# A fused attention and two-layer MoE kernel: the soft dispatch of a token tile issued with the routing logits of the next, 12 places for tile outputs, and block exchanges through DRAM done in place

## The chip, the cores and the metric

The kernel runs on one core of one Trainium2 chip. The metric is the device time of one launch in microseconds; the median of 3 runs before the change is 968.15 us.

## The reference

Three stages in float32. Block-causal attention runs over 8 batches, 8 heads, 576 positions and a head width of 64 (blocks of 64). A dense layer pair follows on 4608 tokens, with ELU between, and then a soft mixture of experts with 32 slots:

```python
attn = softmax(where(mask, scale * q @ k.T, -1e9)); x = concat_heads(attn @ v)
h = x @ w_in
x = where(h > 0, h, exp(min(h, 0)) - 1) @ w_out
logits = x @ phi
d = softmax(logits, axis=tokens);  slot_input = d.T @ x
slot_out[e] = relu(slot_input[e] @ w1[e]) @ w2[e]
out = softmax(logits, axis=slots) @ slot_out
```

## The kernel before, in words

The work is 32 **pairs** (two heads of one batch, numbered `n`) and 36 **tiles** of 128 tokens (numbered `i`); four pairs feed four and a half tiles. Nothing is a loop over all of it at run time: each step is recorded with `add` (engine or engines, a guessed duration, what it reads and writes, a key), and `Plan.order` (L126) replays the records once at build time as a list scheduler over guessed durations. It takes ready steps by the smallest key and so fixes the order of instructions on every engine. On the chip the order is static: an instruction that is not ready holds up all that stands behind it on its engine. The calls at the end (L1140 on) give keys: a tile every `T` = 22, pairs from a `base` that `EARLY` moves ahead.

TensorE (PE) works in four arrangements of its array, which the plan calls modes: F (128x128; the main matmuls, transposes, small sums), R (64 rows; attention scores), C (64 columns; attention times V) and D (32 columns; routing logits and dispatch).

**A tile.** `tile_split` halves the activations into high and low parts. `tile_range` (L787, four times with `r` = 0 to 3) does 12 matmuls of 512 columns (L795 to L797), exponent on ACT (L800), two DVE steps (L802, L805), and writes ELU outputs into one of 8 places of 512 columns, `gslot`. The output weights are folded into the routing matrix and the slot inputs (`g @ w_out` is applied after dispatch), so only `g` and its transpose are needed. For tiles below 30 DVE transposes blocks of 32x32 into `TT` (L813). `tile_turn` (L823) then exchanges the blocks: per half a tile one DMA writes `TT` to DRAM and four bring it back, each for 32 partitions, into another buffer `GT`. `tile_routing` (L832) reads `GT`: 16 matmuls in mode D into bank POST. `tile_dispatch` (L847) makes the softmax parts out of them on DVE, ACT and PE (L855 to L886) and at the end issues the dispatch, 4 matmuls in mode D into the same bank (L893), added to `ACC` by DVE (L897).

**A pair.** Pairs from 8 on transpose the attention weights in two ways (`pair_swap`, L668). DVE transposes 256 columns of each of six units (L678) into `TU`; one DMA to DRAM and four back exchange the blocks into `PX`. The other blocks, 13 of 128x128, are transposed by PE (L359) in four groups, into PSUM banks PTB and GTB in turn, and copied out by ACT or DVE (L335, L337). `swapped_values` (L723) multiplies by V in mode C (L734), 16 matmuls over 1600 columns, counted for both heads side by side.

The tail (from L931) loads the expert weights in pieces of 1 MB into slots that attention, tiles and first-layer weights give back.

Of the kernel before, what the change touches and what calls it, by code (L numbers as in the profile page):

```python
# [28 lines left out]
TLAG, LATE, NTP = 2.5, 30, 8  # L29
EARLY = 8.0  # L30
# [208 lines left out]
def attention_moe_kernel(ctx: ExitStack, tc, q, k, v, w_in, w_out, phi, w1, w2, consts, out):  # L239
# [25 lines left out]
    TT = ga.take(PIECE)  # L265
    PAD = TT
    NPT = 2
    PTW = 4 * CHS + S
    XW, YW = 12 * 32, 3 * P + 320 + 192
    PT = aa.take(max(2 * NPT * PTW, 16 * XW + 4 * YW))  # L270
    TU, PX, PY = PT, PT + 8 * XW, PT + 16 * XW
# [96 lines left out]

    def gtk(hf):
        return [("gt", hf, b) for b in range(4)]  # L370


    def start():
# [86 lines left out]
        def give_back():  # L460
            add(CP2, cpdur(512), lambda e: copy(e, f(WP, 512), pb(GTB, 512)), r=["gtb"], w=["wp"], key=KWOUT)
            for j, (_, _, keys) in enumerate(raws):
                handover(keys, [("stage", j)])
            handover(["c"], [("wot", 0), ("wot", 1)])
            for hf in range(2):
                handover([("tt", hf, r) for r in range(2)], [("narrow", 2 * hf), ("narrow", 2 * hf + 1)])
# [196 lines left out]
    NEAR = (0, P, 2 * P, 2 * P + 320, 2 * P + 512)  # L663

    def swap_keys(sl):
        return [("px", sl, m) for m in range(4)] + [("py", sl, g) for g in range(4)]

    def pair_swap(n, half, key):  # L668

        sl = n % 2  # L670
        tu, px, py = TU + 4 * XW * sl, PX + 4 * XW * sl, PY + 2 * YW * sl
        if n == NTP and half == 0:
            handover([("tu", y, x) for y in range(2) for x in UNITS] + swap_keys(0) + swap_keys(1), [x for y in range(NPT) for x in pt_keys[y]])
        for x in HALVES[half]:
            if x == "b" or x[0] == 0:
                continue
            o = f(tu, 4 * XW).rearrange("p (m h c u j) -> p h u c m j", m=4, h=2, c=2, j=32)[:, x[1], x[0] - 1]
            add("DVE", 0.1 + 256 / 960, lambda e, x=x, o=o: nc.vector.transpose(  # L678
                out=o, in_=f(pat(x, n), 256).rearrange("p (c m i) -> p c m i", c=2, m=4)),
                r=[pkey(x, n)], w=[("tu", sl, x)], key=key)  # L680
        both = f(py, 2 * YW).rearrange("p (h w) -> p h w", h=2)
        groups = (
            [("b", c) for c in range(4)],
            [((3, h), c) for h in range(2) for c in (2, 3)],
        ) if half == 0 else (
            [((2, 0), 2), ((2, 1), 2), ((0, 0), 0), ((0, 1), 0)],
            [("b", 4)],
        )
        for gi, blocks in enumerate(groups):
            g = gi + 2 * half  # L690
            tb, tk = ((PTB, "ptb"), (GTB, "gtb"))[g % 2]
# [6 lines left out]
            def evac(e, g=g, tb=tb):  # L698
                if g == 0:
                    src = pb(tb, 512).rearrange("p (c h x) -> p h c x", c=4, h=2)  # L700
                    copy(e, both[:, :, P:2 * P].rearrange("p h (c x) -> p h c x", c=2), src[:, :, 0:2])
                    copy(e, both[:, :, NEAR[2] + 256:NEAR[2] + 320], src[:, :, 2])
                    copy(e, both[:, :, NEAR[3] + P:NEAR[3] + 192], src[:, :, 3])
                elif g == 1:
                    src = pb(tb, 512).rearrange("p (h c x) -> p h c x", h=2, c=2)
                    for c in range(2):
                        copy(e, both[:, :, NEAR[2 + c] + P * (1 - c):NEAR[2 + c] + P * (1 - c) + P], src[:, :, c])
                elif g == 2:
                    src = pb(tb, 512).rearrange("p (t h x) -> p t h x", t=2, h=2)
                    copy(e, both[:, :, NEAR[2]:NEAR[2] + P], src[:, 0])  # L710
                    copy(e, both[:, :, 0:P], src[:, 1])
                else:
                    copy(e, both[:, :, NEAR[4]:NEAR[4] + 64], pb(tb, P).rearrange("p (h x) -> p h x", h=2))
            add(*evict(n, (560, 530, 530, 128)[g]), evac, r=[tk], w=[("py", sl, g)], key=key)
# [3 lines left out]
        load(via, f(tu, 4 * XW), 4 * P * 4 * XW, r=[("tu", sl, x) for x in UNITS], w=[("pvia", sl)], key=key, lag=TLAG)  # L718
        for m in (0, 2, 1, 3):
            load(f(px, 4 * XW, 32 * m, 32 * m + 32).rearrange("i (a y) -> i a y", a=4),  # L720
                 via.rearrange("(a i) (m y) -> m i a y", a=4, m=4)[m], 4 * 32 * 4 * XW, r=[("pvia", sl)], w=[("px", sl, m)], key=key, lag=TLAG)

    def swapped_values(n, key):  # L723
# [3 lines left out]
        px = f(PX + 4 * XW * sl, 4 * XW).rearrange("p (a h c u j) -> p h c u a j", a=4, h=2, c=2, j=32)  # L727
        both = f(PY + 2 * YW * sl, 2 * YW).rearrange("p (h w) -> p h w", h=2)
        ring = XR + RING * p + S * (b % 2)

        def pv(e):
# [4 lines left out]
            for c in range(2):  # L736
                go(PVB, 384, c, lambda h: px[:, h, c], c == 0, False)
                go(PVB + 384, 64, c, lambda h: both[:, h, P + 64 * c:P + 64 * c + 64], False, False)
            for c in range(2, 5):
                w = S - P * c  # L740
                go(PVB + 448 - w, w, c, lambda h: both[:, h, NEAR[c]:NEAR[c] + w], False, c == 4)
# [28 lines left out]
    gslot = [(G + 512 * j, ("g", j)) for j in range(NG)]  # L770
    tslot = [(GT + 512 * j, gtk(j // 2)) for j in range(4)]
# [15 lines left out]
    def tile_range(i, r, hb, gs, ts, kr):  # L787
# [21 lines left out]
        if ts is None:  # L809

            hf = r // 2
            tt = f(TT + 1024 * hf, 1024).rearrange("p (b c j) -> p c b j", b=4, j=32)[:, 4 * (r % 2):4 * (r % 2) + 4]
            add("DVE", 0.7, lambda e: nc.vector.transpose(out=tt, in_=f(g, 512).rearrange("p (c b i) -> p c b i", c=4, i=32)),  # L813
                r=[gk], w=[("tt", hf, r % 2)], key=kr)
# [8 lines left out]
    def tile_turn(i, hf, kp):  # L823

        via = turned[hf]
        load(via, f(TT + 1024 * hf, 1024), 1 << 19, r=[("tt", hf, r) for r in range(2)], w=[("via", hf)], key=kp, lag=TLAG)
        for b in (0, 2, 1, 3):
            load(f(GT + 1024 * hf, 1024, 32 * b, 32 * b + 32).rearrange("i (a x) -> i a x", a=4),
                 via.rearrange("(a i) (b x) -> b i a x", a=4, b=4)[b], 1 << 17, r=[("via", hf)],
                 w=[("gt", hf, b)], key=kp, lag=TLAG)  # L830

    def tile_routing(kp):  # L832
        def lg(e):
            for c in range(16):
                j = c % 4
                gt = f(GT + 1024 * (c // 8), 1024).rearrange("p (a c j) -> p c a j", a=4, j=32)[:, c % 8]
                mm(pb(POST, P, 32 * j, 32 * j + 32), lhsT=f(WP + NS * c, NS), rhs=gt, start=(c < 4), stop=(c >= 12))  # L837
        add("PE", 0.9, lg, mode="D", r=["wp"] + gtk(0) + gtk(1), w=["post"], key=kp, load=0.25)
# [8 lines left out]
    def tile_dispatch(tiles, gs, banks, lps, dtx, dx, kp):  # L847
# [42 lines left out]
        def disp(e):  # L890
            for t in range(n):
                for j in range(4):
                    mm(pb(bank, 512, 32 * j, 32 * j + 32), lhsT=f(dx[0] + NS * t, NS), rhs=f(gs[t][j][0], 512),  # L893
                       start=(t == 0), stop=(t == n - 1))
        add("PE", 0.88 * n, disp, mode="D", r=[dx[1]] + [gs[t][j][1] for t in range(n) for j in range(4)], w=[bk], key=kp, load=0.25)
# [4 lines left out]

    def moe_tile(i, key):
        gs = [gslot[(4 * i + r) % NG] for r in range(4)]
# [5 lines left out]
        if i < LATE:  # L908
            tile_routing(key + 17)
        else:  # L910
            for r in range(4):
                tile_logits(r, tslot[r], POST, "post", key + 17)
        tile_dispatch([i], [gs], [(POST, "post")], [(LPS, "lps")], (DTX, "dtx"), (DX, "dx"), key + 17)
# [17 lines left out]
    def tail(key):  # L931
        att = [(nm, s, a) for nm in ("rq", "rk") for s in range(2) for a in range(4)] + [(nm, s) for nm in ("qt", "kt") for s in range(2)] + \
              [("v", s, j) for s in range(NV) for j in range(3)] + [pkey(x, s) for x in UNITS for s in range(2)] + \
              [x for s in range(NPT) for x in pt_keys[s]] + [("tu", s, x) for s in range(2) for x in UNITS] + swap_keys(0) + swap_keys(1)
# [263 lines left out]
```

## Time and profile before

| | before |
|---|---|
| median of 3 runs | 968.15 us (967.9 to 970.31) |
| the profiled execution | 968.03 us, of it a span of 966.0 us |
| PE busy | 925.7 us |
| DVE, ACT, POOL busy | 664.3, 452.5, 275.7 us |
| DMA packets | 261279, 198.62 MB |
| granted clock of TensorE | 0.986 over the span |

The span runs from the first to the last instruction. Busy times of engines overlap each other. A matmul of float32 stands in the trace as two records, so counts of PE records are about twice the matmuls. The duration of a single matmul includes its way through the array, which the next one shares; how far apart successive matmuls start is read from the chain.

### The profile page before, as it was taken

The numbers are of one execution on the slowest core, as the hardware profiler recorded it, in microseconds if no ns is written. First come the engines' busy times: TensorE is split into PE (matmuls) and PEld (weight loads), VectorE is DVE, ScalarE is ACT, GpSimd is POOL, SyncE is SP. The second block draws the span as 40 slices with busy tenths as digits, with TensorE's granted clock in tenths as the row PEclk, the third lists the DMA queues.
The fourth block names the chain that finished last, engine by engine and source line by source line (L and its number), as shares of the span: only waits on it lengthen the run. The fifth ranks groups of instructions, "written<-read, shape, count | busy, mean of one in ns | idle before, by whom it ended". The sixth has DMA issues, their size and how long they took to land.

```text
span 966.0 us, 19123 instructions
## 1 busy us (share of the span) xinstructions
PE 925.7 (96%) x6708; PEld 630.0 (65%) x6708; DVE 664.3 (69%) x1739; ACT 452.5 (47%) x1336; POOL 275.7 (29%) x428
## 2 busy tenths in 40 slices
PE   8889999999999999999999999999999999999992
PEld 6556777666666666666666667667667666766351
DVE  5877795677777777777788787787777744443151
ACT  5865655454544544544444444444444433332143
POOL 2863442143332322333323323333333211000000
PEclk9989999999999999999999999999999999999996
DMA  9945756748776777867867788777755579058969
GB/s 237 251 112 163 214 191 179 157 119 215 205 207 191 201 202 211 194 179 201 212 191 199 190 211 194 196 202 206 212 169 168 175 239 379 16 189 304 368 223 354
DMA packets 261279, 198.62 MB, mean 206 GB/s; under 512 B 180544, under 2 KB 223680, under 8 KB 261184
## 3 DMA queue, kind: packets, MB, share of 16 engines
q1 hardware_dynamic: 259984, 197.11, 71.6%
q8 instruction: 53, 0.87, 0.4%
q10 hardware_dynamic: 1200, 0.30, 0.1%
q14 instruction: 42, 0.34, 0.1%
HBM read 133.38 MB, written 63.96 MB: 204 GB/s over the span
## 4 chain that ended last, share of the span: by engine, by line
PE 82%; DMA 5%; DVE 4%; POOL 2%; issue 2%; ACT 2%; SPq 1%; ACTq 0%; DVEq 0%; POOLq 0%
PE ps L795 14%; PE ps L797 13%; PE ps L796 13%; PE ps L359 9%; PE ps L572 8%; PE ps L734 7%; PE ps L893 3%; PE ps L837 3%; PE ps L564 2%; POOL att L603 2%; DMA att<-in_moe_w_dram 1%; DVE g L427 1%; PE ps L1064 1%; PE ps L456 1%; PE ps L762 1%
## 5 line engine op out<-in xcount | busy, mean ns | idle before, releaser
L603 POOL TENSOR_SCALAR att<-att,base 128x128 f32<-128x128 f32 (+4 forms) x288 | 184.4, 659 | 262.5 <-DVE base L599 161.0
L795 PE MATMUL ps<-w,xhl 128*128 128x512 f32 x576 | 253.0, 439 | 0.0
L797 PE MATMUL ps<-w,xhl 128*128 128x512 f32 x576 | 227.2, 395 | 0.9 <-POOL xhl L782 0.9
L796 PE MATMUL ps<-w,xhl 128*128 128x512 f32 x576 | 225.9, 392 | 0.0
L586 ACT ACTIVATE att<-ps,base 128x128 f32<-128x128 f32 (+4 forms) x288 | 157.8, 554 | 94.7 <-DVE base L583 80.4
L583 DVE TENSOR_REDUCE base<-ps 128x1 f32<-128x128 f32 (+4 forms) x288 | 135.3, 501 | 25.2 <-PE ps L568 15.9
L800 ACT ACTIVATE xe<-ps 128x512 f32<-128x512 f32 x144 | 86.3, 599 | 116.3 <-PE ps L797 114.8
L795 PEld LDWEIGHTS ps<-w,xhl 128*128 128x128 f32 x576 | 109.1, 189 | 48.4 <-issue 27.0
L335 ACT COPY att<-ps 128x256 f32<-128x256 f32 (+3 forms) x241 | 86.0, 409 | 113.4 <-PE ps L359 109.5
L797 PEld LDWEIGHTS ps<-w,xhl 128*128 128x128 f32 x576 | 108.0, 188 | 26.3 <-POOL xhl L782 1.7
L796 PEld LDWEIGHTS ps<-w,xhl 128*128 128x128 f32 x576 | 108.9, 189 | 14.8
L802 DVE TENSOR_SCALAR xe<-xe 128x512 f32<-128x512 f32 x144 | 66.4, 461 | 72.9 <-ACT xe L800 70.5
L359 PE MATMUL ps<-base,att 128*128 128x128 f32 x592 | 99.3, 284 | 11.1 <-POOL att L603 8.9
L805 DVE TENSOR_TENSOR g<-xe,ps 128x512 f32<-128x512 f32 x144 | 98.1, 682 | 3.5
L359 PEld LDWEIGHTS ps<-base,att 128*128 128x128 f32 x592 | 70.1, 144 | 46.0 <-issue 16.4
L572 PE MATMUL ps<-att 64*128 64x128 f32 (+3 forms) x512 | 95.7, 468 | 1.2 <-ACT att L586 1.2
L782 POOL TENSOR_TENSOR xhl<-xe,xhl 128x512 fp32r<-128x512 f32 x36 | 46.6, 1297 | 147.1 <-ACT xhl L780 132.9
L813 DVE STREAM_TRANSPOSE g<-g 128x512 f32<-128x512 f32 x120 | 83.0, 694 | 3.7 <-PE ps L359 1.5
L734 PE MATMUL ps<-att 128*64 128x64 f32 (+4 forms) x768 | 71.0, 337 | 0.1
L572 PEld LDWEIGHTS ps<-att 64*128 64x128 f32 x512 | 41.6, 185 | 37.7 <-issue 17.5
L734 PEld LDWEIGHTS ps<-att 128*64 128x64 f32 x768 | 43.3, 137 | 31.7 <-issue 23.6
L678 DVE STREAM_TRANSPOSE att<-att 128x256 f32<-128x256 f32 x144 | 57.4, 416 | 2.8 <-POOL att L603 2.7
(130 smaller groups left out, 1072.0 us busy)
## 6 DMA issues: line engine op xcount, KB each, us to landing
turned<-g SPq DMA_DIRECT2D x60, 512.0 KB, 3.2
g<-turned SPq DMA_DIRECT2D x240, 128.0 KB, 3.4
swapped<-att SPq DMA_DIRECT2D x24, 768.0 KB, 4.2
att<-swapped SPq DMA_DIRECT2D x96, 192.0 KB, 3.9
att<-in_moe_w_dram SPq DMA_DIRECT2D x11, 1024.0 KB, 11.7
att<-in_v_dram SPq DMA_DIRECT2D x64, 128.0 KB, 3.0
g<-in_moe_w_in_dram SPq DMA_DIRECT2D x16, 512.0 KB, 5.2
w_late<-in_moe_w_dram SPq DMA_DIRECT2D x8, 1024.0 KB, 6.6
```

What stands on the lines that cost most here:

```text
L335: nc.scalar.copy(o, i)
L359: mm(o, lhsT=i, rhs=f(IDN + base, n, base, base + n), start=True, stop=True, is_transpose=True)
L572: mm(pb(at((u, h)), P * (u + 1)), lhsT=f(qt + P * u, P, 64 * h, 64 * h + 64), rhs=f(kt, P * (u + 1), 64 * h, 64 * h + 64), start=True, sto ...
L583: add("DVE", 0.08 + wide(x) / 960, lambda e, x=x, c=c: nc.vector.tensor_reduce(out=f(c, 1), in_=pb(at(x), wide(x)), axis=AX.X, op=ALU.max, ...
L586: add("ACT", 0.50 + wide(x) / 1300, lambda e, x=x, c=c: nc.scalar.activation(f(pat(x, n), wide(x)), pb(at(x), wide(x)), AF.Exp, bias=f(c, ...
L603: add("POOL", (0.28 + wide(x) / 1050) * (1.3 if n < 8 else 1.0), lambda e, x=x, p=p: nc.gpsimd.tensor_scalar(out=f(p, wide(x)), in0=f(p, w ...
L734: mm(pb(o, w, 64 * h, 64 * h + 64), lhsT=f(vs + 320 * h + D * c, D), rhs=rhs(h), start=start, stop=stop)
L795: mm(pb(bank, 512), lhsT=fr(xh + P * kk, P), rhs=hi, start=(kk == 0), stop=False)
L796: mm(pb(bank, 512), lhsT=fr(xh + P * kk, P), rhs=lo, start=False, stop=False)
L797: mm(pb(bank, 512), lhsT=fr(xl + P * kk, P), rhs=hi, start=False, stop=(kk == 3))
L800: add("ACT", 0.48, lambda e: nc.scalar.activation(f(ee, 512), pb(bank, 512), AF.Exp), r=[("h", hb)], w=[("e", hb)], key=kr)
L805: add("DVE", 0.6, lambda e: nc.vector.tensor_tensor(out=f(g, 512), in0=f(ee, 512), in1=pb(bank, 512), op=ALU.max), r=[("e", hb), ("h", hb) ...
```

## The change

Tile outputs get 12 places from tile 5 on (`gmore`, four of them in space that the pairs no longer use). From tile 5 to 29 `tile_dispatch` ends without its dispatch; the dispatch of tile i-1 is issued by `tile_routing` of tile i, right behind the 16 logit matmuls, into bank GTB. That is so for 24 tiles; the dispatch of tile 29 is issued by itself during tile 30. `TT` and `GT` both serve as transpose buffers, for even and odd tiles, and the exchange brings blocks back into the buffer they came from: the blocks on the diagonal stay, and the 12 others come back in six DMAs in place of four (`MOVES`). Pairs do the same with `PX`, with 16 blocks in place of 12: DVE transposes three blocks of units 2 and 3 and two of unit 1, and PE transposes 9 blocks in place of 13, in three groups, all into PTB. The part of V's matmul with 320 columns is cut in 256 and 64. `EARLY` puts the pairs after the eighth up to 16 ahead in place of 8.

```diff
-EARLY = 8.0
+TLAG, LATE, NTP, JOINED = 2.5, 30, 8, 5
+EARLY = 16.0
...
-    XW, YW = 12 * 32, 3 * P + 320 + 192
+    XW, YW = 16 * 32, 2 * P + 320
...
+    MOVES = ((0, 1, 4), (2, 0, 2), (1, 2, 4), (3, 0, 3), (1, 0, 1), (2, 3, 4))
...
-            o = f(tu, 4 * XW).rearrange("p (m h c u j) -> p h u c m j", m=4, h=2, c=2, j=32)[:, x[1], x[0] - 1]
-            add("DVE", 0.1 + 256 / 960, lambda e, x=x, o=o: nc.vector.transpose(
+            cs = min(x[0] + 1, 3)
+            o = f(px, 4 * XW).rearrange("p (m b j) -> p b m j", m=4, j=32)[:, at:at + step * (cs - 1) + 1:step]
+            add("DVE", 0.12 + P * cs / 960, lambda e, x=x, o=o, cs=cs: nc.vector.transpose(
...
-            [((3, h), c) for h in range(2) for c in (2, 3)],
-            [((2, 0), 2), ((2, 1), 2), ((0, 0), 0), ((0, 1), 0)],
-            [("b", 4)],
+        groups = ([("b", c) for c in range(4)], [((3, 0), 3), ((3, 1), 3), ("b", 4)]) if half == 0 else ([((0, 0), 0), ((0, 1), 0)],)
...
-            tb, tk = ((PTB, "ptb"), (GTB, "gtb"))[g % 2]
+            tb, tk = (PTB, "ptb")
...
-        load(via, f(tu, 4 * XW), 4 * P * 4 * XW, ...)
-        for m in (0, 2, 1, 3):
-            load(f(px, 4 * XW, 32 * m, 32 * m + 32)...)
+        load(via, f(px, 4 * XW), 4 * P * 4 * XW, ...)
+        for j, (m, a0, a1) in enumerate(MOVES):
+            load(f(px + XW * a0, XW * (a1 - a0), 32 * m, 32 * m + 32)...)
...
+    gmore = gslot + [(spare + 512 * j, ("g", NG + j)) for j in range(4)]
+    def outputs(i):
+        at = gmore if JOINED <= i < LATE else gslot
+        return [at[(4 * i + r) % len(at)] for r in range(4)]
...
-        load(via, f(TT + 1024 * hf, 1024), 1 << 19, ...)
-        for b in (0, 2, 1, 3):
-            load(f(GT + 1024 * hf, 1024, 32 * b, 32 * b + 32)...)
+        via, o, sl = turned[hf], TG[i % 2] + 1024 * hf, i % 2
+        load(via, f(o, 1024), 1 << 19, ...)
+        for j, (b, a0, a1) in enumerate(MOVES):
+            load(f(o + 256 * a0, 256 * (a1 - a0), 32 * b, 32 * b + 32)...)
...
-    def tile_routing(kp):
+    def tile_routing(i, kp):
+        before = outputs(i - 1) if i > JOINED else []
         def lg(e):
             for c in range(16):
...
+            if before:
+                slots_of([i - 1], [before], GTB, (DX, "dx"))
...
+        if before:
+            gathered(1, GTB, "gtb", kp)
...
+        if later:
+            return
+        tile_gather(tiles, gs, bank, bk, dx, kp)
...
-        base = T * 4.5 * (b - 1) + 24.0 * p - 24.0 - (EARLY if n >= NTP else 0.0) if b else KAS * p + KA0
+        base = T * 4.5 * (b - 1) + 24.0 * p - 24.0 - (min(EARLY, 8.0 + 4.0 * (n - NTP)) if n >= NTP else 0.0) if b else KAS * p + KA0
```

`slots_of` holds the four dispatch matmuls and `gathered` the DVE step that adds them to `ACC`; both are as before.

How the instructions move is shown at three places. On PE before, around the dispatch of a tile in mid-program (L893 is the dispatch, L564 the first scores of a pair, L359 transposes):

```order
L795 MATMUL ps<-w_68,xhl 128x512
L796 MATMUL ps<-w_68,xhl 128x512
L797 MATMUL ps<-w_68,xhl 128x512
L359 MATMUL ps<-base 128x128
L795 MATMUL ps<-w_68,xhl 128x512
L796 MATMUL ps<-w_68,xhl 128x512
L797 MATMUL ps<-w_68,xhl 128x512
L893 MATMUL ps<-g,base 32x512 x4
L564 MATMUL ps<-att,base 128x288 x2
L795 MATMUL ps<-w_68,xhl 128x512
```

The dispatch stands by itself, with mode F on both sides; the logits of the same tile (L837) stand 22 rows ahead of it.

On PE now, at V's matmul, the logits (L853), the dispatch (L919) and the transposes of a pair (L360); L880 and L881 are the small sums that were L859 and L860:

```order
L739 MATMUL ps<-att 64x256 x2
L739 MATMUL ps<-att 64x64 x2
L739 MATMUL ps<-att 64x192 x2
L739 MATMUL ps<-att 64x64 x2
L853 MATMUL ps<-g,base 32x128 x16
L919 MATMUL ps<-att,base 32x512 x4
L360 MATMUL ps<-base,att 128x128 x4
L568 MATMUL ps<-att,base 128x288 x2
L360 MATMUL ps<-base,att 128x128 x3
L880 MATMUL ps<-base 128x128
L881 MATMUL ps<-base 128x32
L808 MATMUL ps<-w_71,xhl 128x512
```

The dispatch follows the logits with no other mode between, and the pair's first two groups of transposes, 4 and 3, have only two score matmuls between them.

On SP (the queue that issues the DMAs) now, at a pair's exchange and that of half a tile:

```order
L355 DMA swapped_75<-att 128x2048
L355 DMA turned_77<-g 128x1024
L355 DMA att<-swapped_75 32x3x512
L355 DMA att<-swapped_75 32x2x512 x2
L355 DMA att<-swapped_75 32x3x512
L355 DMA att<-swapped_75 32x512 x2
L355 DMA g<-turned_77 32x3x256
L355 DMA g<-turned_77 32x2x256 x2
L355 DMA g<-turned_77 32x3x256
L355 DMA g<-turned_77 32x256 x2
```

Each of the two returns is six DMAs, where four stood before.

## Rows read from the trace of the kernel before

**Rows 1.** Page, part 1: busy us (share of the span) xinstructions.

```profile
PE 925.7 (96%) x6708; PEld 630.0 (65%) x6708; DVE 664.3 (69%) x1739; ACT 452.5 (47%) x1336; POOL 275.7 (29%) x428
```

**Rows 2.** Windows: stretch, length, busy (x records) per engine, granted clock, DMA share, GB/s.

```profile
core 0: us, PE busy (x) PEld busy (x) DVE busy (x) ACT busy (x) POOL busy (x), PEclk, DMA share, GB/s
0.00:175.00 175.00, 160.40 (x1261) 116.45 (x1262) 129.23 (x310) 107.87 (x288) 79.94 (x102) 0.97 0.69 192
175.00:886.00 711.00, 705.35 (x4964) 485.80 (x4962) 511.65 (x1389) 320.54 (x1003) 195.79 (x326) 1.00 0.71 197
886.00:966.00 80.00, 59.92 (x489) 27.75 (x488) 23.41 (x42) 24.12 (x46) 0.00 (x0) 0.90 0.86 316
```

**Rows 3.** Waits of PE, 180 to 860 us: us in total, times, longest; all but one row.

```profile
PE ps L359 <- DVE g L805: 1.5, 2, 1.4
PE ps L359 <- ACT base L868: 0.9, 1, 0.9
PE ps L797 <- POOL xhl L782: 0.9, 2, 0.6
PE ps L359 <- ACT att L335: 0.8, 1, 0.8
```

**Rows 4.** Chain that ended last, 500 to 516 us: start, us to the next piece, what.

```profile
500.16 2.87 PE ps L734 x32
...
504.34 0.44 PE ps L359 x4
...
507.52 0.23 PE ps L797
507.76 1.01 PE ps L837 x32
508.77 0.43 PE ps L795
509.20 0.23 PE ps L796
...
514.01 0.99 PE ps L893 x8
515.01 0.43 PE ps L795
```

**Rows 5.** The same chain, V's matmul of a pair below 8.

```profile
146.04 0.27 PE ps L758 x4
146.30 2.59 PE ps L762 x20
```

**Rows 6.** The same chain, a long run of D-mode matmuls of the tail.

```profile
896.00 7.00 PE ps L1042 x64
```

**Rows 7.** Groups by form, 250 to 750 us, DVE: busy, mean ns, idle before.

```profile
L813 DVE STREAM_TRANSPOSE g<-g 128x512 f32<-128x512 f32 x93 | 64.6, 695 | 1.5
L678 DVE STREAM_TRANSPOSE att<-att 128x256 f32<-128x256 f32 x122 | 48.6, 416 | 2.8 <-POOL att L603 2.7
L337 DVE COPY att<-ps 128x256 f32<-128x256 f32 x22 | 8.2, 408 | 1.4 <-PE ps L359 1.4
L337 DVE COPY att<-ps 128x128 f32<-128x128 f32 x13 | 3.5, 283 | 0.5 <-PE ps L359 0.4
```

**Rows 8.** Groups by form, 250 to 750 us, ACT.

```profile
L800 ACT ACTIVATE xe<-ps 128x512 f32<-128x512 f32 x92 | 55.1, 599 | 84.1 <-PE ps L797 83.9
L335 ACT COPY att<-ps 128x256 f32<-128x256 f32 x81 | 27.2, 377 | 59.0 <-PE ps L359 59.0
L335 ACT COPY att<-ps 128x128 f32<-128x128 f32 x49 | 11.5, 280 | 9.3 <-PE ps L359 9.2
```

**Rows 9.** Timeline of SP's issues: start, us, what, number.

```profile
520.82 1.74 SPq L354 DMA_DIRECT2D att<-swapped  x4
522.67 1.79 SPq L354 DMA_DIRECT2D g<-turned  x4
```

**Rows 10.** Waits of SP's queue, 200 to 800 us: us in total, times, longest.

```profile
SPq L354 <- DMA turned<-g: 49.0, 29, 5.0
SPq L354 <- DMA swapped<-att: 24.6, 13, 4.0
```

**Rows 11.** Timeline of SP, loads of expert weights ahead of the tail.

```profile
797.90 6.41 SPq L964 DMA_DIRECT2D att<-in_moe_w_dram  x6
804.37 44.01 SPq L964 DMA_DIRECT2D xe<-in_moe_w_dram  x2
```

More of the change, by code (lines that the diff above doesn't have):

```diff
@@ L268, in attention_moe_kernel @@
     PTW = 4 * CHS + S
[L269 to L271 removed]
+    XW, YW = 16 * 32, 2 * P + 320
+    PT = aa.take(max(2 * NPT * PTW, 8 * XW + 4 * YW))
+    PX, PY = PT, PT + 8 * XW
     RQ = aa.take(2 * S)
@@ L367, in handover, with tgk @@
             plan.readers.setdefault(b, []).extend(sorted(ops))
+    def tgk(s, hf):
+        return [("tg", s, hf, j) for j in list(range(6)) + ["a", "b"]]
     def gtk(hf):
-        return [("gt", hf, b) for b in range(4)]
+        return tgk(1, hf)
     def start():
@@ L465, in give_back @@
             for hf in range(2):
-                handover([("tt", hf, r) for r in range(2)], [("narrow", 2 * hf), ("narrow", 2 * hf + 1)])
+                handover(tgk(0, hf), [("narrow", 2 * hf), ("narrow", 2 * hf + 1)])
         for j in range(16):
@@ L845, in tile_logits, with tile_dispatch @@
         add("PE", 0.25, lg, mode="D", r=["wp"] + ts[1], w=[bk], key=kp, load=0.25)
-    def tile_dispatch(tiles, gs, banks, lps, dtx, dx, kp):
+    def tile_dispatch(tiles, gs, banks, lps, dtx, dx, kp, later=False):
         n = len(tiles)
@@ L888, in tile_dispatch, with slots_of, gathered @@
             r=["alpha", "tsum"], w=["ssum"], key=kp + 0.2)
[L890 to L895, printed above, removed]
+        if later:
+            return
+        tile_gather(tiles, gs, bank, bk, dx, kp)
+    def slots_of(tiles, gs, bank, dx):
+        n = len(tiles)
+        for t in range(n):
+            for j in range(4):
+                mm(pb(bank, 512, 32 * j, 32 * j + 32), lhsT=f(dx[0] + NS * t, NS), rhs=f(gs[t][j][0], 512),
+                   start=(t == 0), stop=(t == n - 1))
+    def gathered(n, bank, bk, kp):
         for x in range(0, 512, 512 // n):
@@ L899, in tile_dispatch, with tile_gather @@
                 r=["alpha", bk], w=["acc"] if n == 1 else [("acc", x // 256)], key=kp)
+    def tile_gather(tiles, gs, bank, bk, dx, kp):
+        n = len(tiles)
+        add("PE", 0.88 * n, lambda e: slots_of(tiles, gs, bank, dx), mode="D", r=[dx[1]] + [gs[t][j][1] for t in range(n) for j in range(4)],
+            w=[bk], key=kp, load=0.25)
+        gathered(n, bank, bk, kp)
     def moe_tile(i, key):
-        gs = [gslot[(4 * i + r) % NG] for r in range(4)]
+        gs = outputs(i)
+        if i == JOINED:
+            handover([k for _, k in gmore[NG:]], [x for y in range(NPT) for x in pt_keys[y]])
         tile_split(i, key - 6)
@@ L949, in tail @@
         slots = [(flat(PT + PIECE * j), att) for j in range(10)]
-        slots += [(flat(TT), [("tt", j, r) for j in range(2) for r in range(2)])]
+        slots += [(flat(TT), tgk(0, 0) + tgk(0, 1))]
         slots += wslot[:1] + [(ring(hf), xk[hf]) for hf in range(2)] + wslot[1:]
```

90 lines of the change are left out of this document (46 added, 44 removed).

## The prediction

> **What bounds the kernel now.** I read the busy times first: PE is busy for 925.7 us of the span of 966.0, the next engine, DVE, for 664.3 [rows 1]. A mean over the span doesn't say where, so the windows come next. From 175 to 886 us PE is busy for 705.35 of 711.00 us at full granted clock (1.00, so 2.4 GHz) [rows 2]; it pauses for 5.65 us in all. The start is different (160.40 of 175.00), and so is the tail (59.92 of 80.00). The waits of PE bear the middle out: from 180 to 860 us it waited 4.5 us, in pieces of at most 1.4 us, the four largest of them shown [rows 3]; no DMA is among what it waited for. In the middle, then, the only thing that shortens the kernel is less work on PE, and every wait on another engine or queue is free as long as PE doesn't meet it. The chain of waits, read in order of time, gives what a piece of PE's work costs there, since each piece ends where the next begins [rows 4].
>
> **The change part by part.**
>
> *Fewer transposes on PE.* 13 blocks of a pair become 9, for 24 pairs: 96 transposes less. Four in a row took 0.44 us [rows 4], 0.11 us each; so 96 x 0.11 = 10.6 us less.
>
> *The dispatch behind the logits.* A dispatch between two stretches of mode F cost 0.99 us, and the main matmul behind it 0.43 where one in a run takes 0.23 [rows 4]. The same kind and size of matmul in one long run of mode D, 32 of them, took 7.00 us, or 0.875 for four [rows 6]. So going in costs 0.99 - 0.875 = 0.115 us and coming out 0.43 - 0.23 = 0.20 us. The logits pay both too (1.01 us, then 0.43), and go on paying. The joined dispatch pays neither: 0.315 us for each of 24 tiles, 7.6 us. The program's order agrees in number: the changes between the four modes on PE fall from 402 to 354, by 48, which is one in and one out for each of 24.
>
> *The 320 columns cut in two.* V's matmul of a pair becomes 18 matmuls in place of 16, over the same 1600 columns. Pairs below 8 do those 1600 columns in 12 matmuls, for 0.27 + 2.59 = 2.86 us [rows 5], and later ones in 16 for 2.87 us [rows 4]. Four more cost 0.01 us, so the 48 more here cost 0.1 us, and I take 0. The Trainium skill (TensorEngine Tiling (Array Packing), Instruction Overhead) says that each matmul has about 60 cycles of overhead. By that page 48 matmuls would cost, as an estimate at 2.4 GHz, 1.2 us, and the gain would be smaller by that much; the two rows that differ in nothing but the number of matmuls show none of it.
>
> *DVE.* A pair's six transposes of 256 columns (416 ns) become four of 384 and two of 256. No row has 384; it lies between 416 and the 695 ns of 512 columns [rows 7], near 555, their middle. That adds 4 x 0.139 = 0.56 us a pair, 13.4 us in all. From the order, DVE loses 14 copies of 256 columns and 9 of 128: 14 x 0.408 + 9 x 0.283 = 8.3 us less [rows 7]. The net is 5 us on 511.65 of 711 [rows 2], hidden behind PE. ACT has 51 instructions less and is hidden anyhow.
>
> *SP.* The two ways back take six DMAs in place of four: 60 half tiles and 24 pairs, 168 more issues. Four took 1.74 and 1.79 us [rows 9], 0.44 each; so 74 us more on SP's queue. Four pairs and 4.5 tiles, the repeating unit, had 109 issues, 48 us, and now have 135, 59 us. A unit takes 98 us: 92 exponent passes in 500 us, four a tile [rows 8], are 21.7 us a tile. From 200 to 800 us the queue also waited 73.6 us for the first half of an exchange to land [rows 10], some 12 us a unit. 71 of 98 us still fit, with PE as the cover. The bytes hardly change: a half tile's way back falls by a quarter, a pair's way out grows by a third.
>
> *Places, buffers, `EARLY`.* Twelve places keep the outputs until the later dispatch; two transpose buffers in turn part one tile from the next; pairs come up to 8 key units earlier. All this moves work about under PE's cover: 0, and if that cover goes, it is on the side of fewer waits. The tail needs the pair's space back, and now also the last late dispatch. Six of its loads were issued by 804.3 us, and two further ones then took the queue until 848 [rows 11], so some us of delay there are covered by 40.
>
> *The one place where I see cover shrink* is bank PTB. All three groups of a pair go through it, and between the first two the new order has about 1 to 1.4 us of PE work. The bank is emptied by two copies of ACT, between 0.28 and 0.6 us each (the 128-column copy, and a full 512-column pass of ACT as upper end [rows 8]). ACT stood idle for 59.0 us ahead of 81 such copies [rows 8], so it is usually there on time: 0.7 to 0.9 us, under the cover. I take 0; at the upper end, with ACT busy with one pass of 0.60 us first, PE would wait 0.35 us a pair, 8.4 us in all.
>
> **The sum**: 10.6 + 7.6 = 18.2 us. The profiled execution took 968.03 us, of it 966.0 of span; 968.03 - 18.2 = 949.8, and the median lies 0.12 above that execution: **949.9 us**.
>
> **The rivals.**
>
> 1. *PTB holds PE up*, at the upper end above: 949.9 + 8.4 = 958.3 us. For it: one bank where there were two. Against: ACT's idle time, and that PE waited for ACT's copies only 0.8 us in the whole middle [rows 3].
>
> 2. *The longer way over DVE reaches PE.* Each pair's 0.56 us lies ahead of its DMA; if all came through, 13.4 us, 963.3 us. The Trainium skill (VectorE: DVE Perf Modes, Rules for kernel authors) advises TensorE for a 128x128 transpose if PSUM will do as the place for it; by that page this part goes the wrong way. The traces bear it out only where DVE is short of time, and it is busy for 72% of the middle against PE's 99% [rows 2].
>
> 3. *Slower: SP's queue comes too late.* It works in order, and each exchange ends two issues, 0.88 us, later. Of 30 tiles and 24 pairs the last exchange stands ahead of the logits or of V's matmul. If all 54 came through, PE would wait 47.5 us: 949.9 + 47.5 = 997.4. From 18.2 / 54 = 0.34 us an exchange the gain is gone. For it: the queue already waits for landings, and is now taken for 72% of the time. Against: PE waited for no DMA before, and the pairs come earlier.
>
> 4. *The joined dispatch saves nothing*, if PE empties between logits and dispatch although the mode stays. Then 10.6 us remain: 957.5. Against it: the run of 32 in the tail changes weights for each matmul and stays at 0.875 us for four [rows 6].
>
> **How the numbers follow.** The forecast has 0.67, with a range of its own of 944 to 955: the lower end gives back the 5.65 us of pauses, the upper end half of what rival 1 or 4 costs. Rivals 1 and 4 have 0.10 and 0.05, rival 2 has 0.06. Rival 3 has 0.08 for a result beyond its point of decision, and 0.04 stay for a gain and a loss that cancel. Faster is the forecast with rivals 1, 2 and 4: 0.88; same 0.04 (within 0.3%, 2.9 us, about what a measurement of this kernel can tell from no change); slower 0.08. The range goes from 943, a little below all pauses gone (944.2), to 962, over rivals 1 and 4 and most of rival 2.
>
> **What would show each step.** In the profile after, the PE transposes of `att` blocks should have 96 records less and still 0.44 us for four in the chain; the dispatch should stand behind the logits there with about 0.87 us and no 0.43 between; the middle should again show PE over 98% busy. A wait of PE's transposes on ACT's copies shows rival 1, on DVE's transposes rival 2, a wait of logits or V's matmul on a DMA rival 3, a dispatch of 0.99 us behind the logits rival 4. The prediction is wrong if PE's busy time falls by 18 us and the span doesn't, or if the start, where PE isn't the bound, grows.

## The result, and the profile after

The change took 956.44 us in the median of 4 runs (955.77 to 960.66), against 968.02 (964.87 to 970.31) for the kernel before on the same chip. The ratio is 0.9899, with an interval of 0.9866 to 0.9931: by the ratio 9.8 us (6.7 to 13) of the 18.2 that were forecast, about half. The time lies inside the range and outside the range that the forecast itself had (944 to 955). In the profiled execution the span fell from 966.0 to 954.0 us, by 12.0, within that interval.

The busy times of the page (part 1) answer to [rows 1]:

```profile
PE 908.7 (95%) x6708; PEld 623.3 (65%) x6708; DVE 675.9 (71%) x1718; ACT 439.4 (46%) x1285; POOL 272.6 (29%) x428
```

PE is busy 17.0 us less, and the span is 12.0 us shorter: 5.0 us of new idle time on PE. The windows, cut as in [rows 2] with the same start and the same length of tail, say where:

```profile
0.00:175.00 175.00, 161.90 (x1281) 116.27 (x1281) 133.60 (x314) 106.66 (x284) 79.48 (x102) 0.99 0.69 190
175.00:874.00 699.00, 686.94 (x4943) 479.29 (x4944) 519.22 (x1367) 308.49 (x955) 193.14 (x326) 1.00 0.68 199
874.00:954.00 80.00, 59.85 (x488) 27.70 (x488) 23.09 (x39) 24.23 (x46) 0.00 (x0) 0.90 0.85 312
```

The tail is what it was. The middle is 12.0 us shorter; PE is busy there for 18.4 us less, of which 1.5 us is work that now lies before 175 us (the granted clock of the start was 0.97 then and is 0.99 now, so this part need not be the change's). Its pauses rose from 5.65 to 12.06 us, by 6.4. The granted clock of the middle is 1.00 (2.4 GHz), as before. So the work went nearly as forecast, 17.0 us over the span, and about a third of it came back as waits. The waits of PE from 170 to 850 us (in total, times, longest), to be read beside [rows 3], name them:

```profile
PE ps L808 <- DVE g L818: 5.5, 6, 2.0
PE ps L808 <- DVE att L818: 2.2, 3, 1.0
PE ps L360 <- DVE base L924: 0.9, 1, 0.9
PE ps L739 <- DMA att<-swapped: 0.7, 2, 0.5
PE ps L880 <- DVE base L876: 0.4, 2, 0.2
PE ps L739 <- DMA g<-turned: 0.4, 2, 0.2
```

L808 is the first matmul of a tile range (L795 before), L818 the second DVE step of ELU (L805 before), which empties the PSUM bank that a later range writes. Nine such waits hold 7.7 us. The two rows on DMAs come to 1.1 us, and there is none on ACT's copies of transposes.

One of the nine, on PE and DVE in order of time (start, us, what, in brackets the idle time before it and its releaser):

```profile
495.38 0.39 PE L810 MATMUL ps<-w,xhl 128*128 128x512 f32 x1
496.53 0.50 PE L808 MATMUL ps<-w,xhl 128*128 128x512 f32 x1 [0.77 <-DVE att L818]
```

```profile
493.70 0.43 DVE L815 TENSOR_SCALAR xe<-xe 128x512 f32<-128x512 f32 x1 [0.48 <-ACT xe L813]
494.05 1.01 DVE L587 TENSOR_REDUCE base<-ps 128x1 f32<-128x384 f32 x2
495.39 0.49 DVE L587 TENSOR_REDUCE base<-ps 128x1 f32<-128x128 f32 x2 [0.33 <-ACT att L590]
495.80 0.68 DVE L818 TENSOR_TENSOR att<-xe,ps 128x512 f32<-128x512 f32 x1
```

Between the two ELU steps stand four maxima over a pair's scores (L587), and ahead of the second two DVE waits 0.33 us for an exponent of ACT. L818 has all it needs from 494.1 us on, and starts at 495.80. PE finds its bank still taken. DVE is no bottleneck here, with 0.48 us idle just before: the fixed order has put the step that PE needs behind steps that it doesn't need.

Seven of the nine waits, 4.8 us, have maxima ahead of an ELU step in this way. The other two have another cause. At 426.29 us PE waits 0.90 us because the exponent on ACT came late (DVE was idle for 1.99 us ahead of L815). At 214.51 us it waits 1.97 us, the longest, and there the ELU steps stand behind the addition of a tile that still dispatches by itself (L924), for which DVE was idle for 1.54 us:

```profile
211.98 0.75 DVE L924 SCALAR_TENSOR_TENSOR base<-base,ps 128x512 f32<-128x512 f32 x1 [1.54 <-PE ps L919]
212.64 1.04 DVE L815 TENSOR_SCALAR xe<-xe 128x512 f32<-128x512 f32 x1
213.69 0.19 DVE L584 MEMSET ps<- 64x64 f32 x2
213.79 0.66 DVE L818 TENSOR_TENSOR g<-xe,ps 128x512 f32<-128x512 f32 x1
```

The chain of waits shows the two terms of the sum (start, us to the next piece):

```profile
335.76 2.88 PE ps L739 x36
338.64 1.01 PE ps L853 x32
...
380.18 1.01 PE ps L853 x32
381.19 0.86 PE ps L919 x8
...
783.62 0.44 PE ps L360 x4
```

The dispatch (L919) stands right behind the logits (L853) and takes 0.86 us; alone it took 0.99 [rows 4]. V's 18 matmuls (36 records) take 2.88 us, where 16 took 2.87. Four transposes still take 0.44 us, and PE has 496 records of transposes in all where it had 592, 96 less.

### The profile page after: what moved, and what is told of

Same layout as the page of the kernel before. It is cut to its first block, busy times and chain, and to the rows that moved or that the text cites. A ratio compares the mean times of both kernels' runs of the same rounds, so it can differ in the third digit from the quotient of the medians.

```text
span 954.0 us, 19403 instructions
## 1 busy us (share of the span) xinstructions
PE 908.7 (95%) x6708; PEld 623.3 (65%) x6708; DVE 675.9 (71%) x1718; ACT 439.4 (46%) x1285; POOL 272.6 (29%) x428
## 4 chain that ended last, share of the span: by engine, by line
PE 74%; DVE 8%; DMA 7%; SPq 4%; ACT 2%; issue 2%; POOL 1%; ACTq 0%; DVEq 0%; POOLq 0%
PE ps L808 13%; PE ps L810 11%; PE ps L809 11%; PE ps L360 8%; PE ps L576 7%; PE ps L739 7%; SPq L355 4%; PE ps L919 3%; PE ps L568 2%; PE ps L853 2%; DMA att<-swapped 2%; DMA swapped<-att 2%; PE ps L767 2%; DVE base L587 2%; PE ps L460 1%
## 5 line engine op out<-in xcount | busy, mean ns | idle before, releaser
L808 PE MATMUL ps<-w,xhl 128*128 128x512 f32 x576 | 249.8, 434 | 7.8 <-DVE g L818 5.5
L607 POOL TENSOR_SCALAR att<-att,base 128x128 f32<-128x128 f32 (+4 forms) x288 | 181.0, 647 | 222.2 <-DVE base L603 151.0
L587 DVE TENSOR_REDUCE base<-ps 128x1 f32<-128x128 f32 (+4 forms) x288 | 135.7, 503 | 21.3 <-PE ps L572 12.2
L808 PEld LDWEIGHTS ps<-w,xhl 128*128 128x128 f32 x576 | 108.8, 189 | 52.0 <-issue 19.1
L336 ACT COPY att<-ps 128x128 f32<-128x128 f32 (+3 forms) x192 | 75.7, 434 | 95.8 <-PE ps L360 90.6
L815 DVE TENSOR_SCALAR xe<-xe 128x512 f32<-128x512 f32 x144 | 68.1, 473 | 67.0 <-ACT xe L813 65.6
L360 PE MATMUL ps<-base,att 128*128 128x128 f32 (+1 forms) x496 | 83.2, 282 | 9.7 <-POOL att L607 8.5
L360 PEld LDWEIGHTS ps<-base,att 128*128 128x128 f32 (+1 forms) x496 | 58.0, 143 | 44.5 <-POOL att L607 17.6
L795 POOL TENSOR_TENSOR xhl<-xe,xhl 128x512 fp32r<-128x512 f32 x36 | 46.3, 1291 | 133.1 <-ACT xhl L793 127.0
L818 DVE TENSOR_TENSOR g<-xe,ps 128x512 f32<-128x512 f32 x108 | 73.3, 680 | 2.4
L689 DVE STREAM_TRANSPOSE att<-att 128x384 f32<-128x384 f32 x144 | 70.4, 507 | 5.3 <-POOL att L607 4.2
L739 PEld LDWEIGHTS ps<-att 128*64 128x64 f32 x864 | 46.8, 137 | 32.3 <-issue 23.6
L826 DVE STREAM_TRANSPOSE g<-g 128x512 f32<-128x512 f32 x84 | 58.0, 695 | 1.7 <-DMA turned<-g 0.2
```

The source lines that it names most:

```text
L336: nc.scalar.copy(o, i)
L360: mm(o, lhsT=i, rhs=f(IDN + base, n, base, base + n), start=True, stop=True, is_transpose=True)
L587: add("DVE", 0.08 + wide(x) / 960, lambda e, x=x, c=c: nc.vector.tensor_reduce(out=f(c, 1), in_=pb(at(x), wide(x)), axis=AX.X, op=ALU.max, ...
L607: add("POOL", (0.28 + wide(x) / 1050) * (1.3 if n < 8 else 1.0), lambda e, x=x, p=p: nc.gpsimd.tensor_scalar(out=f(p, wide(x)), in0=f(p, w ...
L739: mm(pb(o, w, 64 * h, 64 * h + 64), lhsT=f(vs + 320 * h + D * c, D), rhs=rhs(h), start=start, stop=stop)
L808: mm(pb(bank, 512), lhsT=fr(xh + P * kk, P), rhs=hi, start=(kk == 0), stop=False)
```

## The experiments

They were made to tell where the 6.4 us of waits come from, and what each part of the change is worth alone. Every time is given as a ratio to the kernel before, run on the same chip, with its interval; 0.001 is about 1 us. Pauses are length less PE's busy time in the middle, from 175 us to 80 us before the end.

**Without the join.** The dispatch goes back behind its own tile, and with it the tile outputs go back to 8 places (the 12 hang on the same number); the rest stays, in an order that the plan makes anew.

```diff
-TLAG, LATE, NTP, JOINED = 2.5, 30, 8, 5
+TLAG, LATE, NTP, JOINED = 2.5, 30, 8, 30
...
-            if i == LATE:
-                tile_gather([i - 1], [outputs(i - 1)], GTB, "gtb", (DX, "dx"), key + 4)
```

> The change without the joined dispatch and without the 12 places: each tile dispatches by itself, as before; everything else as in the change. All theories: PE's busy time in the middle rises by 7.6 us against the change (24 times 0.315 us). They differ on PE's waits in the middle, 12.1 us in the change against 5.7 before. Theory A (the longer DVE transposes make DVE late with the ELU steps that free PE's banks): the waits stay at 10 to 14 us, and the time is 6 to 9 us above the change, about 963 to 965. Theory C (the joined dispatch puts its DVE addition ahead of the ELU steps): the waits fall to about 6 us, and the time is only 1 to 3 us above the change, about 958.

963.06 us (9 runs), ratio 0.9963 (0.9944 to 0.9981). The windows row of the middle:

```profile
175.00:881.40 706.40, 694.24 (x4936) 475.40 (x4934) 515.28 (x1363) 310.62 (x953) 192.52 (x326) 1.00 0.67 196
```

PE is busy for 7.3 us more than in the change, where the second term had 7.6. Some 1.5 us of this is, by an estimate, not work: behind the pause at 213.23 us the granted clock was 0.66 for 4.5 us here, and 1.00 at the same place in the profile of the change (the last section has its row):

```profile
213.20:217.70 4.50, 4.47 (x14) 3.41 (x14) 4.20 (x10) 1.02 (x4) 1.98 (x6) 0.66 0.51 148
```

Join and places are worth 0.0064 of ratio, 6.2 us (with both intervals, 2.6 to 9.8). But the pauses are 12.2 us without them too, and the waits on the ELU step 6.8. The join, and the DVE step that adds its result, did not bring them.

**Twice, and less, of DVE's transposes.** In the first kernel two of the four transposes of 384 columns of a pair are done twice; in the second all four are cut to 256 columns from the third such pair on, so the third block is left out. The order of all other instructions is that of the change in both.

```diff
+            if x[0] == 3:
+                add("DVE", 0.0, lambda e, x=x, o=o, cs=cs: nc.vector.transpose(...))
```

> The change with two more DVE transposes of 384 columns a pair (a repetition of those of units (3,0) and (3,1)), 1.1 us a pair, 26 us in all; the order of all other instructions on every engine is the same. Theory A (DVE's work ahead of the ELU steps reaches PE): PE's waits in the middle rise from 12 us to 22 or more, and the time by 8 to 20 us. Theory B (the plan's guesses are too short whatever DVE's load, and DVE has slack, 74% busy): waits rise by less than 4 us, the time by less than 4.

```diff
+            ct = cs if n < NTP + 2 else 2
-                out=o, in_=f(pat(x, n), P * cs)...
+                out=o[:, 0:ct], in_=f(pat(x, n), P * ct)...
```

> The change with the four transposes of 384 columns of a pair cut to 256 from the third such pair on, in the same order of instructions on every engine; the third block of units 2 and 3 is left out of the transposition, so attention is computed with stale blocks there. DVE does 3 blocks a pair less, 0.14 us each of four, 12 us in all. Theory A: PE's waits in the middle fall from 12 us to 6 to 8, and the time by 4 to 6 us, to 951. Theory B: the waits stay above 10 us, and the time within 2 us of the change.

The doubled one took 967.64 us (11 runs), ratio 1.0011 (0.9997 to 1.0025), the lighter one 955.37 (4 runs), 0.9885 (0.9856 to 0.9915). The middle of the first, then of the second:

```profile
175.00:886.30 711.30, 691.36 (x4948) 479.79 (x4945) 540.93 (x1416) 308.97 (x955) 193.11 (x326) 1.00 0.66 195
```

```profile
175.00:873.10 698.10, 686.88 (x4954) 478.93 (x4954) 510.65 (x1369) 308.54 (x955) 193.34 (x326) 1.00 0.68 199
```

With 21.7 us more of DVE in the middle the pauses rise to 19.9 us; with 8.6 us less they fall only from 12.1 to 11.2. The waits of the lighter kernel:

```profile
PE ps L809 <- DVE g L819: 5.3, 6, 2.0
PE ps L809 <- DVE att L819: 1.9, 3, 1.0
```

They are the same nine, 7.2 us in place of 7.7. So DVE's slack is used up (what is added now costs about half its length, 10.8 us by the ratios for 21.7), but the longer transposes are not what the waits come from: at this order, taking them out gives 1.4 us back by the ratios, which the intervals don't tell from nothing.

**The plan's guesses.** Eleven guessed durations of ACT and DVE steps are set to what the trace shows, for instance:

```diff
-        add("ACT", 0.48, lambda e: nc.scalar.activation(f(ee, 512), pb(bank, 512), AF.Exp),
+        add("ACT", 0.60, lambda e: nc.scalar.activation(f(ee, 512), pb(bank, 512), AF.Exp),
...
-        add("DVE", 0.335, lambda e: nc.vector.tensor_scalar(
+        add("DVE", 0.46, lambda e: nc.vector.tensor_scalar(
```

> The change with the scheduler's guesses for eleven steps of DVE and ACT in a tile (the two ELU steps, exponent, maxima of scores, the small routing steps, the addition of the dispatch) set to the durations of the trace; no instruction is added or taken away, the order changes. Theory B (the plan places the next range of PE ahead of the ELU step that frees its bank, because its guesses are short): PE's waits on the ELU step fall from 7.7 us to under 3, and the time by 4 to 6 us, to about 951. Theory A alone: waits fall by less than 3 us, since DVE's load is the same, the time within 2 us of the change.

971.34 us (12 runs), 1.0042 (1.0027 to 1.0058): slower than the change by 0.0143, some 14 us. The pauses are 23.0 us, the waits on the ELU step 13.9. Neither theory had that. A plan with truer numbers in some places is not a better order; the theory that the guesses alone explain the waits falls in this form. With all durations true it was not tried.

**The ELU steps first.** Behind the plan, L815 and L818 are moved ahead of maxima that don't need to precede them, about 30 times, on DVE alone; the other engines' order stays.

```diff
+        for i in self.first:
+            p = next(j for j, x in enumerate(items) if x[0] == i)
...
+                    if items[q][0] not in self.maxima or items[q][2] < ready - 0.2:
+                        break
...
+                items.insert(to, items.pop(p))
```

> The change with one thing moved: on DVE the two ELU steps of a tile go ahead of maxima of a pair's scores that stand before them, where the plan has them ready by then; about 20 places. The order on PE, ACT, POOL and SP is the same, and no instruction is added or taken away. Theory E (PE's added waits are for a bank of a tile that is freed late because its ELU step stands behind maxima in DVE's order): the waits of the main matmuls on the ELU step fall from 7.7 us to 2 to 4, PE's waits in the middle from 12 us to 7 to 9, and the time falls by 3 to 5 us. Theory F (the waits are where DVE's load as such is too high): the same work in another order moves the waits elsewhere, to the scores' exponents and the matmuls behind them; the time stays within 1.5 us.

955.92 us (6 runs), 0.9881 (0.9858 to 0.9904). The middle:

```profile
175.00:872.20 697.20, 686.00 (x4941) 480.09 (x4943) 515.20 (x1368) 308.62 (x955) 193.51 (x326) 1.00 0.69 199
```

DVE at the place that was shown above:

```profile
491.65 0.43 DVE L835 TENSOR_SCALAR xe<-xe 128x512 f32<-128x512 f32 x1 [0.47 <-ACT xe L832]
492.11 0.69 DVE L839 TENSOR_TENSOR att<-xe,ps 128x512 f32<-128x512 f32 x1
492.72 1.02 DVE L606 TENSOR_REDUCE base<-ps 128x1 f32<-128x384 f32 x2
```

The second step now follows the first, and PE's wait there is gone. The waits of this kernel (its lines lie some 20 further down; L839 is L818, L593 the pair's scores, L609 the exponent behind the maxima):

```profile
PE ps L827 <- DVE g L839: 3.8, 3, 2.0
PE ps L593 <- ACT att L609: 1.7, 3, 0.8
PE ps L901 <- DVE base L897: 1.3, 2, 1.0
```

The waits on the ELU step are halved, 7.7 to 3.8 us: six of the seven that stood behind maxima are gone, so the place in DVE's order is what made these. Left are one of the seven (0.93 us) and the two with another cause (1.97 and 0.90 us). But the maxima now come later, ACT behind them, and PE's scores wait for that: the pauses fall by 0.9 us only, to 11.2, and the time can't be told from the change. For the waits theory E had it right; pauses and time are nearer to theory F. So the order of these steps says where PE waits; that another order would give the 6.4 us back is not shown.

**PE's own work put back.** Four of the nine transposes of each pair are done twice on PE, at the same order: the 96 transposes that the change had saved.

```diff
+                if len(blocks) < 4:
+                    for j, (x, c) in list(enumerate(blocks))[:2]:
+                        transpose(pb(tb + P * j, P), f(pat(x, n) + P * c, P))
```

> The change with four transposes a pair repeated on PE, in the second and third group (the same blocks to the same places, so the results are the same); the order of everything else is the same. That is the PE work that the change took away, 96 x 0.11 = 10.6 us. If PE bounds the middle everywhere, the time rises by 10 to 11 us. If the shorter PE work has uncovered DVE's chain (the waits are what is left of PE's missing work), part of it fills waits: the time rises by 5 to 8 us, and PE's waits in the middle fall from 12 us to about 8.

968.35 us (10 runs), 1.0011 (0.9987 to 1.0034): 0.0112 above the change, 10.8 us (with both intervals, 6.9 to 14.7), against 10.6 in the first term. The middle:

```profile
175.00:887.40 712.40, 700.90 (x5058) 491.71 (x5057) 521.62 (x1370) 308.91 (x955) 193.99 (x326) 1.00 0.67 195
```

The pauses are 11.5 us and the waits on the ELU step 7.4. The price of a transpose, 0.11 us, agrees with the measurement, and the waits are not holes that PE's missing work has left: put the work back, and they stay.

**How early the pairs come.** The change with 8 and with 24 in place of 16, and the kernel before with 16.

```diff
-EARLY = 16.0
+EARLY = 8.0
```

> The change with the pairs at most 8 ahead, as before, in place of 16; PE's work is the same, the order of all engines changes. Theory E with the earlier pairs as its cause (their maxima get the smaller keys and so go ahead of the ELU steps): PE's waits on the ELU step fall from 7.7 us to under 3, and the time by 3 to 6 us. Otherwise (the earlier pairs serve the exchanges): the waits of V's matmul on DMAs rise from 1.1 us to 5 or more, and the time by 3 us or more.

> The change with pairs up to 24 ahead in place of 16 (8 gave PE's middle 24.2 us of waits, 16 gives 12.1). If more distance keeps helping, the waits fall to 8 us or less and the time by 3 us or more; if the waits are now those of the tiles' own ELU steps, they stay between 10 and 14 us and the time within 3 us of the change.

```diff
-EARLY = 8.0
+EARLY = 16.0
...
-        base = T * 4.5 * (b - 1) + 24.0 * p - 24.0 - (EARLY if n >= NTP else 0.0) if b else KAS * p + KA0
+        base = T * 4.5 * (b - 1) + 24.0 * p - 24.0 - (min(EARLY, 8.0 + 4.0 * (n - NTP)) if n >= NTP else 0.0) if b else KAS * p + KA0
```

> The kernel before with one part of the change alone: pairs up to 16 ahead in place of 8, in the same steps. PE's work is that of before. If the earlier pairs alone bring the added waits of PE on the ELU step (7.7 us in the change, none of them in the middle of the kernel before), they appear here: PE's waits in the middle rise from 5.7 to 10 us or more and the time by 4 us or more. If the earlier pairs only serve the change's longer exchanges, the waits stay at 4 to 8 us and the time within 2 us of the kernel before.

| | ratio (interval) | pauses of the middle |
|---|---|---|
| the change, 8 | 1.0072 (1.0050 to 1.0094) | 24.2 us |
| the change, 16 | 0.9899 (0.9866 to 0.9931) | 12.1 us |
| the change, 24 | 0.9919 (0.9892 to 0.9945) | 11.2 us |
| before, 16 | 0.9970 (0.9955 to 0.9984) | 2.0 us |

This number alone, in the kernel before, is worth 0.0030, 2.9 us, and leaves almost no pause:

```profile
175.00:878.30 703.30, 701.28 (x4915) 484.98 (x4916) 514.99 (x1401) 315.33 (x984) 193.71 (x325) 1.00 0.70 198
```

In the change it decides: with 8, the rest of the change is slower than the kernel before. Neither theory had the reason. It is not that V's matmul waits for DMAs (2.5 us, in one wait); the waits on the ELU step rise from 7.7 to 13.1 us:

```profile
PE ps L808 <- DVE att L818: 7.7, 8, 1.9
PE ps L808 <- DVE g L818: 5.4, 4, 2.0
```

And an earlier start is not what brought the waits, since the kernel before with 16 has none of them. With 24 they are 8.3 us, and the time can't be told from that with 16.

**The exchanges.** First four DMAs a return, with the diagonal blocks brought back too; then the change with the tile's exchange as it was, from `TT` to `GT`.

```diff
-    MOVES = ((0, 1, 4), (2, 0, 2), (1, 2, 4), (3, 0, 3), (1, 0, 1), (2, 3, 4))
+    MOVES = ((0, 0, 4), (2, 0, 4), (1, 0, 4), (3, 0, 4))
```

> The change with four DMAs back for an exchange in place of six: whole strips, the blocks on the diagonal too (the same values come back), so 168 issues less on SP, 74 us of its queue, and a third more bytes back. If SP's longer queue costs time (waits of V's matmul on DMAs, 1.1 us, and late inputs behind other waits), the time falls by 1 to 4 us. If SP's queue is covered, it stays within 1.5 us, but for what the changed order of the plan does.

```diff
-        via, o, sl = turned[hf], TG[i % 2] + 1024 * hf, i % 2
-        load(via, f(o, 1024), 1 << 19, ...)
-        for j, (b, a0, a1) in enumerate(MOVES):
-            load(f(o + 256 * a0, 256 * (a1 - a0), 32 * b, 32 * b + 32)...)
+        via = turned[hf]
+        load(via, f(TT + 1024 * hf, 1024), 1 << 19, ...)
+        for b in (0, 2, 1, 3):
+            load(f(GT + 1024 * hf, 1024, 32 * b, 32 * b + 32)...)
...
```

> The change with the exchange of tiles as before: one transpose buffer, another to come back to, four DMAs; pairs, joined dispatch and places as in the change. PE's work is that of the change. If the exchange in place (120 more issues on SP, DVE's transposes waiting for the logits two tiles before) brings the added waits, PE's waits in the middle fall from 12 to 6 to 8 us and the time by 4 to 6 us. If it is what keeps tiles apart, the waits rise to 15 or more and the time by 3 us or more.

With four DMAs 962.59 us (5 runs), 0.9943 (0.9920 to 0.9966): the 168 issues that SP is spared gain nothing, and the time is 4.3 us longer (0.3 to 8.3). The DMA share of the middle is 0.79 where the change has 0.68, but the plan's order on every engine is another one too, so the time is not shown to come from the bytes. With the old tile exchange 961.75 us (10 runs), 0.9950 (0.9935 to 0.9965): 4.9 us longer (1.4 to 8.5), pauses 14.5 us, and 8.1 us of waits on the ELU step, so the exchange in place did not bring them:

```profile
PE ps L808 <- DVE g L818: 6.5, 6, 1.4
PE ps L739 <- DMA att<-swapped: 2.9, 1, 2.9
PE ps L808 <- DVE att L818: 1.6, 2, 0.9
```

**Eight places.** The joined dispatch, with outputs in 8 places as before.

```diff
-        at = gmore if JOINED <= i < LATE else gslot
+        at = gslot
```

> The change with 8 places for tile outputs in place of 12. The dispatch of a tile must then be done before the next tile but one writes its outputs. PE's order changes its mode 320 times here, 354 in the change. If the places don't bind, PE saves 34 times 0.16 us, 5 us, and the time falls by 3 to 6 us. If they bind, DVE's ELU steps wait for the dispatch, the matmuls for them, and the time rises by 10 us or more.

1086.69 us (6 runs), 1.1247 (1.1220 to 1.1273). Its middle, and the first and third of its waits:

```profile
175.00:1004.40 829.40, 743.77 (x4954) 511.54 (x4950) 523.33 (x1387) 311.37 (x939) 191.29 (x326) 0.93 0.57 167
```

```profile
PE ps L576 <- ACT att L590: 36.2, 21, 3.2
...
PE ps L853 <- DMA g<-turned: 11.7, 3, 10.9
```

The pauses are 85.6 us, and PE is busy for 56.8 us more than in the change, with a granted clock of 0.93 in place of 1.00. So 8 places bind, and without more there is no join that pays. The way is not the expected one: the main matmuls wait for the ELU step for only 2.8 us, the scores and the logits of the tile wait instead. That a tile's outputs wait for a dispatch which now stands behind the next logits, and that the plan moves the waits from there, is argued and not shown. What four more places do without the join was not tried.

## Why the prediction was right, and where it was wrong

The time lies in the range because the range reached up to 962, over rivals 1 and 4. Neither of these came true; another loss of about that size did, and that it was no larger is luck.

**Right: PE as the bound, and what PE saves.** The two terms were 10.6 and 7.6 us; put back one at a time they measured 10.8 us of time (6.9 to 14.7; 96 transposes) and 6.2 (2.6 to 9.8; the join with its places), the second with 7.3 us of PE's busy time, or, by the estimate above, some 5.8 at the same clock. In sum PE is 17.0 us less busy over the span against 18.2. The chain's rows priced both: 0.44 us for four transposes, and 0.99 against a part of a long run for the dispatch.

**Right: V's matmul at 0.** 18 matmuls take 2.88 us against 2.87 for 16. The Trainium skill (TensorEngine Tiling (Array Packing), Instruction Overhead) gives each matmul about 60 cycles; the two rows are 0.01 us apart, so by the measurement two more matmuls in one run of mode C add next to nothing.

**Right: SP, PTB and the mode.** Rival 3 (SP's queue): PE waits for DMAs for 1.1 us, and four DMAs a return are not faster. Rival 1 (bank PTB): no wait on ACT's copies. Rival 4: the joined dispatch takes 0.86 us, not 0.99.

**Wrong: the cover.** The step that failed is "All this moves work about under PE's cover: 0, and if that cover goes, it is on the side of fewer waits", with the DVE part, "The net is 5 us on 511.65 of 711 [rows 2], hidden behind PE". What was taken as 0 is +6.4 us of pauses. The net itself was too small: DVE is busy for 7.6 us more in the middle and 11.6 over the span. Idle time on DVE was counted as cover, 28% of the middle. But DVE's idle time covers nothing for PE where the step that PE needs stands in DVE's order behind steps that are not ready or not wanted. The prediction priced how long DVE works, and not in which order; the order list was there to be read at L815 and L818, and was looked at on PE and SP only.

Why the waits came with the change, the runs narrow down and don't settle. The waits are there without the join (6.8 us), with the old tile exchange (8.1), with shorter transposes (7.2) and with PE's work put back (7.4); `EARLY` 16 in the kernel before doesn't bring them. What is left, by elimination, is the pairs' new scheme: with it, the early start and the exchange in place, but without the join, the ratio is 0.9963, and the early start alone has 0.9970. So the 10.6 us that PE should save over the pairs are nearly all given back, in pauses that are 10.2 us longer (2.0 to 12.2). That is the difference of two kernels whose tile exchange differs too; the old pair scheme with the rest of the change was not tried. A rival stands: each of these runs but those with one step repeated, shortened or moved has an order of its own from the plan, and the waits may belong to the order that came out and to no one part. That ELU steps stand behind maxima is shown, by the row on DVE and by moving them, for six of the nine waits; why the plan puts them there stays open, and so does the cause of the 6.4 us as a whole.

**Wrong: `EARLY` at 0.** It is worth 2.9 us in the kernel before (1.5 to 4.3) and 16.7 in the change (12.9 to 20.5). The prediction had it as a gain without a size.

**Rival 2** named the right engine with the wrong mechanism. Its time, 963.3, is 6.9 us off; its cause, the longer transposes ahead of the pair's DMA, falls with the lighter kernel. Its point that DVE is busy for 72% only was the reason for its small chance, and the same thought was the forecast's mistake.

Sum, by ratios and in this order of steps: the early start -2.9 us, the pairs and the exchange in place -0.7, the join with its places -6.2, together -9.8. Each part has an interval of 1.4 to 3.6 us either way, so the small middle term may be a few us of either sign; and as the two sizes of `EARLY` show, a part is worth something else in another order of steps.

## What to carry to other kernels

Price what an engine saves from the chain of waits: here 10.6 us for a measured 10.8, with an interval of some 4 us either way. Then ask for each producer that the bound engine waits on not only how busy it is but what stands ahead of it in its engine's fixed order; here this found six of nine waits, though taking them away moved the waits more than it shortened the time. Where a list scheduler makes that order, a change of the work can make a new order everywhere, and its waits belong in the range: here 11 to 24 us in the middle of the change, according to one start time or eleven guesses. Whether a saving and the pauses are tied can be tested by putting the work back at the same order.

## What was not expected of the hardware

Behind a pause of PE the clock can fall, so that the pause costs more than itself, and its length alone doesn't say whether it does. With `EARLY` 8, PE waited 2.53 us for a DMA in the middle of V's matmul; the 32 records behind the pause took 4.34 us up to the next piece, where all 36 take 2.88 in the change:

```profile
404.48 4.41 PE L739 MATMUL ps<-att 128*64 128x384 f32 x32 [2.53 <-DMA g<-turned]
```

```profile
395.00:404.48 9.48, 6.91 (x40) 4.73 (x36) 9.05 (x29) 5.09 (x20) 2.02 (x3) 1.00 0.85 217
404.48:409.00 4.52, 4.52 (x33) 2.57 (x34) 2.50 (x7) 0.07 (x1) 3.83 (x9) 0.62 0.85 205
```

The granted clock was 1.00 up to the end of the pause and 0.62 in the 4.5 us behind it, so most of these at the lower level of 1.2 GHz. The DMAs were as busy as before; DVE and ACT were less so.

The pause of 1.97 us shown above, at the same instructions, is in nine of the profiled executions. In the change it left the clock at 1.00, as it did with the shortened transposes and with the ELU steps first. In the six others the 4.5 us behind it had 0.62 to 0.66. The change, then that with `EARLY` 8:

```profile
214.50:219.00 4.50, 4.49 (x19) 3.67 (x20) 4.47 (x11) 1.46 (x5) 2.00 (x6) 1.00 0.51 149
```

```profile
213.10:217.60 4.50, 4.50 (x13) 3.55 (x14) 4.47 (x11) 1.02 (x4) 2.01 (x6) 0.62 0.52 149
```

By an estimate from the second row, 4.5 us at 0.62 lose 1.7 us. A single profile can have or lack that, so PE's busy time in two profiles compares only to within a few such losses. What decides it no run here shows: a pause of 2.46 us (the plan's guesses) left the clock at 1.00 too.

And a queue with room took six DMAs a return in place of four without a loss that can be seen: with four, 168 issues less and another order of the plan, the kernel was not faster.
